# Block-sparse attention and a gated convolution feed-forward: the middle tap divided out, thirteen relus on another engine

## The chip, the core and the metric

The kernel runs on one core of a Trainium2 chip. A core has a matrix engine (TensorE, PE in the profile, with its weight loads as PEld), a vector engine (VectorE, DVE), a scalar engine that evaluates functions such as exp and tanh (ScalarE, ACT), a general engine (GpSimd, POOL) and a queue engine that here only issues transfers (SyncE, SP). Each engine works through its own list of instructions in the order in which they stand; an instruction that waits for another engine holds back all that stand behind it on its own. The metric is the device time of one execution in microseconds, smaller is better.

## What is computed

Attention over 4 batches, 8 heads, 768 positions and 64 values a head, with a mask of 32-wide blocks, and behind it a feed-forward part in which each of 1024 features is gated by a three-tap convolution along the positions:

```python
h = np.maximum(x @ w_in, 0.0)
conv_out = np.zeros_like(h)
for k in range(3):
    conv_out += conv_w[k][None, None, :] * hp[:, k:k + S, :]     # hp is h with a zero at each end
gate = 1.0 / (1.0 + np.exp(-conv_out))
return (h * gate @ w_out).astype(np.float32)
```

`x` is the attention's result, all heads side by side (512 values), `w_in` is 512 by 1024, `conv_w` 3 by 1024, `w_out` 1024 by 512.

## The kernel before

**Attention.** The work is cut into 144 units of eight 128x128 blocks of scores. A unit's scores are written by TensorE into one of two PSUM tiles `st` (line 746), ScalarE turns them into exponentials in one of eight SBUF tiles `pt` (line 757, the exp), and TensorE multiplies those with the values into one of two PSUM tiles `av` (line 779). A unit's scores can only be written when the exp of the unit two before has read that `st` tile. VectorE divides by the sums (`rcp`, `xtok`, lines 696 and 698), and the result is transposed into `xT`.

**Feed-forward.** The positions are cut into nine segments: seven of 384 positions (two to a batch, the last batch has one), one of 256 and one of 128. For a segment TensorE computes eight feature blocks of 128 features (F1, line 895: four matmuls of 384 columns a block) into one of two PSUM tiles `mix_65` and `mix_66`. A relu reads that tile and writes half of the positive part into the SBUF tile `hE`, either on ScalarE (line 915) or on VectorE (line 917); only then may TensorE write the tile anew. The same two `mix` tiles serve the transposes of queries and keys (lines 470 and 508, read out by the copies of lines 328 and 330) and the output blocks (F2, line 825, read out by copies into `o2s`).

The gate works on pairs of feature blocks, four pairs `pr` a segment, each in a buffer `m`: VectorE multiplies `hE` by each of the three taps (line 949, six instructions a pair, `cw` holds a tap of each feature as a column), adds the three products (line 959, two instructions), ScalarE takes the tanh of half of the sum, both blocks in one instruction (line 998), VectorE adds one (`g1`, line 1001) and multiplies with `hE` (`g2`, line 1006) into `gT`, which F2 reads. The factor one half in `hE` and the one in the tanh make that the sigmoid of the reference; `cw` holds the taps doubled. The segment of 128 positions does its taps on TensorE instead (line 970, tanh in line 975).

**What sets the order.** All operations are written as a graph, with the engines on which each may run. The string `ORDER` names each operation by two characters in the order in which it is put down, with a letter where a choice of engine was made and a character for each buffer; `put_down` follows it and plans nothing itself. So the string fixes the list of each engine, the engine of each relu, and the buffers.

The lines that the change and the steps below touch, shortened:

```python
i = nc.vector.tensor_scalar(out=m_t[cb.index][:, x, y, 0:w], in0=hE_t[heb.index][:, f0 + y, t0 + x:t0 + x + w],
                            scalar1=cw[:, x, f0 + y:f0 + y + 1], scalar2=None, op0=ALU.mult)      # L949
a1 = op("add", {"DVE": t_d2(2 * w)}, add(1, 0), due + 2.2, [m1, m0], uses=[cb])
a2 = op("add", {"DVE": t_d2(2 * w)}, add(1, 2), due + 2.3, [a1, m2], uses=[cb])
```

Of the kernel before, what the change touches and what calls it, by code (L numbers as in the profile page):

```python
# [32 lines left out]
iu18i08j8f38k4ix0iyizV8q18riviwViS4iTiUiV8v08wiA0iBiD1iE8s58x6iCAiFAi+0iW2o22p2qV22rV2u2002v22x2w8A18B7/08F086
878GiG08b8c8g8hiJ1iH8C78H0iXiIA8l8m8t18K18L8S08T8uiK2108yj08n1i/8oj122ViLV23Vj61j28M18U28z8X18Y8D8E8I8J90091
8Z3925j38N8O08ViM1951iP0969769d08WiQiNiOA8+9e8/939i194989j998P2j7iYj8j4iZj98Qj59a3iRVja9bje29f79k1jfjgjhji9n0
9o9p3jE1jbjs09g19s19t9u69h9l9x09yjt9z79mjF9F19q9r9G9v9w9A9K09L9B0jcjdjGjujj9H19M62F2G42C2D02Q2I2H2N2O12R32T2S
2Y2Z22y08222z2J18p8R9c9P19Q9R4jkjljHjIV29C02AV39Djv9I9U09Va019Ja1jN1jOjwA39W0a22jK0jLjMA1jPV0Gk63a50a6aa1jQ19N
abjT0jRk7k8jSVk9jUa75ac3jVA2/30032312Kaf0agak1alah7jZ1j+am1j/A9O9SjW09T9X9Yas0a31ata4a8jXa9ax1ayk31k4ke4kakb0L
kg9Z10H2BVjYVkm0knkf2LV4au6az4aC0aDaE0k00adk1aH1aeaIk2AaiajanaP0aQaJ2jm0jnkh9+ki2MVap2k5Vkcku1aU1aVaR5aW3kjjo
aZ0a+jpao0avawb21b3jy1aAaBaFaGaKaLa/7aqkv2EV32PV4kpkd1kob70b8kqkxaM3kk2+V0aNkwkl9E32U22Vin330jxarit349/b46jqA4  # L40
jzbf1bgb94jAjBbk0kI0aS1blaTaXaYaObh0krbm2jCA1bp1b0bqb1b5kJbu0bvb6ksky2WV02XVktbr5kzkAkBkC1babb0kD373833a3b13f
3c3d3ebw13mbC1bDbc035V1kEkKbH0kFbE3bIbM1bNkLkGV339A1bdkMV036VkO1kPbibJ7bO6kQVbR0bSkR0kSbT4kTVla2lblcldlebW1bj
bXbnbobsbY0kX1c20c3btkU0c71c8c42c95kYkVbxbykWAkZVbz2bAli3cc0cdbF1bGch1cibKl11ce1lfbLl2cp0cj3cqk+0bPbQbUbVbZb+0
cu1ljlklll3Vlmb/1lgc0cr7lnlhloc5l71cvk/l0Alq4cz0c6cacbcfcgcAcw6l40lplrlsltl5l8ckcE1clcFcm3l9VlucB0l6Aly0lzcnlB
lAlC3p3n03q23u3r3s3tcG4cJ0cKcs1ctcxcycClM0cL2lvcR1lG1cDcScW0cT5cHcXcY3cIlNcMcN0lHcUcVc/1d0d40d5lDjDbe03g13hjJ
c1bB3v23wcokHd17lwlxd66cZlIc+lOdc1ddde43iV2lElFd2lP3jVlQV1lJdh0lKA2didj5dm1dnm20m3d3do73E3B3F43J3G3xV3m4V0cO0
cPme1mfmgV3yVdr0d7dsm50m6dw1d8dxdt1m7Vmq1mrmsmtmud913oV23H3T3U33C13Idy03Y3V3W3Q3R23X43443df1mb1dE0dFdG2m80m9mc
dJ1mdAmaAdadKdgdO0dPdL6dQ3mh1mk0mlmidkdT1dUdldpdqdudvmjAd/0e0dzmn1dV4e41e5dA0dHdImoe15e67mpAe90eaeb1mvmy2mmVmz
mG3mImHmJmKmAdB2mBdCmCmO4lS0dMdNdRee1dSefdWdXlTe21e3lY1eg0mLdY3mwmx0mPlUej0eklZl+lVe7l/mDmQdZmRmMmS3DV3mEel2
m0A3e8er1esecew0edehexet6kN3kjr3K03LlR3Z1cQ1lWA0mFn01eieB1eCemn1mN3MV4mTey3eD4mUmV3NVeo0epmW0mXen0mYmZeG0eH  # L50
m+A4n2n3db3+3/V03zlLdDn4V140V3SV4eO1eP3Pd+nf0m1423leq2lX3O3An5ngnc1nd45A0eI5eQ7neAnhVnC0eT0eUeY1eZn90nan61n7
eV1e+0nEnDnbVn8AnFnu1f10f2euevf61f7nl0ezf32nmni1fe0f86nvnGnwnHnxnnVffeAnjeEnkVfj1fkeFeJeKfg3fl4nynzeL1nK2nLeM
nMnIeR1eSeWeXfo0fpno0e/f0ft1fuf4f5fq5f9nr1nsfv7fa0fB0fCnpfhfG1fHfifmfnfrfsfwfxfb2nNnAnJnqVnBntAfcnOfy3nS3fD1
fI0fL0fMfzn+1fN2fT1fUfE1fFo40nTnUnVnWfY0fJfZfKnPfV641eNfdfAf+3nXnQfOn/o5nRg11g2fPfQ0fW0fXf/g90g0g34gao0o6gb5g4
ge1gffRnYnZo7o1o2V2o8A3gg7gj0gkg5om0ong610MooA1gl1op1oqgc1gr1g7orVoK4oMoLoNoOov0gsgt0os1gdowoxAgw0otouAgxgB1gh
gCgioB0gmgnoCgy2oS0go2oDVgpfS3g8o9gqgD6oPgK0oy1ozgLgP1oH0oIgQgu0oAAgM3oE1gvgzgAgEoFgX0gYgR4oJAoGAoToUo+1o/p0p1
oVgFh31gN1gZ5gG3oQgHoWoXog0gOgSohgU0p62h4gI1h80h9gT0oiojp7oYp8oR1p9gVgJApap2h57okA0pq1prhh1g+pz0g/h61pApsApC3
h01ha1pBApbp3oa1h7hbobocodh1pEpDpFhd2pcpdp4oZpt0puhioeA1pvAgW0h2m/hep5pK4pLpw1pxhj0pyAhc0pk0plpmhf1pnhkhlpGpN
p+2p/hm3hnpMq1hgApoA3pHpOpS0pTpIpUpVpJpWpe1pfpgho0phhpApiA4ql0qmqnAqo1qpqi0qz1qAqjpPqqAqB1qkApppjolo3ofqE0qF
qr1qsqu1qvpQqCpRq60q7qDq0pXqtAqw3qG4qxq2q3qypYpZqc1qJ1qKqdqO0qL1qeqHq4qMq5q8q9qNqIqaA3qfqPqQqRqgA4qbqhqSA0qTS  # L60
qU0qVqWqXq+1qYA2qZSq/r0r1r2Ar3A
# [52 lines left out]
def kernel(  # L114
# [22 lines left out]
    SLOT_DMA = 3  # L137
    NF, NPE = 4, 5
    WHOLE = ()
# [29 lines left out]
    m_t = many(NCV, [128, 3, 2, 392], BF16, "m")  # L169
# [6 lines left out]
    cw = sb.tile([128, 3, NFFC], FP32, tag="cw", name="cw")  # L176
    ident = sb.tile([128, 128], BF16, tag="ident", name="ident")
# [195 lines left out]
    for s in range(NHE):  # L373
# [10 lines left out]
        op0=ALU.mult), T(8.5), [o_cwt], uses=[b_cw])  # L384

# [449 lines left out]
    def whole_gate(n, heb, gtb, base, W):  # L835

        got = []
        for f in range(NFFC):
            due = base + W * 0.6 * (f + 1) / 8
            cb = Buf(P_cv)  # L840
            rd = [relu[(n, f)], relu[(n - 1, f)]]

            def m_(x, cb=cb):
                return m_t[cb.index].rearrange("p x y s -> p x (y s)")[:, x, 0:S]

            def mul(x, f=f, m_=m_):
# [28 lines left out]
    for n, (b, g, tok, C, _) in enumerate(SEGS):  # L875
# [194 lines left out]
```

## Time and profile before

| what | value |
|---|---|
| three runs | 204.78, 205.15 and 205.30 us; median 205.15 |
| profiled execution, first to last instruction (span) | 202.8 us (its own device time is not on the page) |
| mean granted TensorE clock | 0.998 |
| PE busy | 196.8 us, 2708 matmuls |
| ACT busy | 189.7 us, 251 instructions |
| DVE busy | 181.8 us, 572 instructions |
| POOL busy | 57.5 us |

The median of the runs lies 2.35 us above the span. Busy time is the time in which an engine has at least one instruction in flight; instructions that follow each other on one engine overlap somewhat, so mean durations times counts come out above it. The row of a group gives, behind the bar, its busy time in us and the mean length of one in ns. A row of the timeline gives the start and the length in us, the engine, the line, what is written from what, and how many instructions in a row were merged.

### The profile page before, as it was taken

To read this page: it belongs to the slowest core of one execution; us is meant where nothing else is said; L and a number is where in the kernel's file an instruction comes from. 1 tells how busy PE (TensorE), PEld (TensorE's weight loads), DVE (VectorE), ACT (ScalarE), POOL (GpSimd) and SP (SyncE) were. 2 spreads that over 40 slices of the span, in tenths; PEclk is the share of its full clock that TensorE was granted. 3 is DMA by queue.
4 is the path that set the end of the run, shared out by engine and by line. 5 is a ranking of instruction groups with operands and counts; after the bars stand their busy time and mean duration, and the time that the engine had idled before them with its cause. 6 is when DMAs were issued, how large, how long until landed. Compare 5 with 4: busy or idle time off the path is not lost.

```text
span 202.8 us, 6814 instructions
## 1 busy us (share of the span) xinstructions
PE 196.8 (97%) x2708; PEld 153.9 (76%) x2708; DVE 181.8 (90%) x572; ACT 189.7 (94%) x251; POOL 57.5 (28%) x112
## 2 busy tenths in 40 slices
PE   7899999999999999999999999999999999999993
PEld 7799977986788777877688877876678877876742
DVE  7999989999999979999899988999899968999950
ACT  6999999999999999999999998999999989998842
POOL 8870568630520354202534328400000000000000
PEclk9999999999999999999999999999999999999999
DMA  6999999999998399956869699994321202001515
GB/s 143 177 223 207 182 135 132 167 171 151 155 122 129 61 141 154 213 106 132 133 108 159 82 197 218 135 176 115 124 72 24 41 14 68 13 10 60 204 63 202
DMA packets 53655, 25.96 MB, mean 128 GB/s; under 512 B 39616, under 2 KB 50584, under 8 KB 53624
## 3 DMA queue, kind: packets, MB, share of 16 engines
q0 software_dynamic: 19984, 11.24, 43.7%
q1 hardware_dynamic: 33208, 13.87, 34.6%
q8 instruction: 21, 0.34, 0.7%
q10 hardware_dynamic: 432, 0.43, 0.6%
q14 instruction: 10, 0.08, 0.1%
HBM read 23.08 MB, written 6.29 MB: 145 GB/s over the span
## 4 chain that ended last, share of the span: by engine, by line
PE 78%; ACT 15%; issue 3%; DVE 2%; DMA 1%; ACTq 0%
PE st L746 25%; PE mix L895 18%; PE mix L825 17%; PE av L779 14%; ACT pt L757 11%; DMA o2s<-in_k_dram 1%; DVE e L330 1%; ACT m L998 1%; PE mix L810 1%; PE st L825 1%; PE av L970 1%; ACT nat L328 1%; PE mix L508 1%; ACT hE L915 0%; ACT o2s L328 0%
## 5 line engine op out<-in xcount | busy, mean ns | idle before, releaser
L757 ACT ACTIVATE pt<-st 128x1024 bf16<-128x1024 f32 x144 | 140.6, 1039 | 1.8 <-PE st L746 0.9
L779 PE MATMUL av<-vt,pt 128*128 128x65 bf16 x1152 | 59.9, 193 | 0.2 <-DVE vt L330 0.2
L779 PEld LDWEIGHTS <-pt 128*128 128x128 bf16 x1152 | 52.3, 97 | 9.9 <-issue 0.3
L895 PE MATMUL mix<-xT,winb 128*128 128x384 bf16 (+2 forms) x288 | 53.6, 308 | 0.1
L949 DVE TENSOR_SCALAR m<-hE,cw 128x382 bf16<-128x382 bf16 (+2 forms) x192 | 49.3, 316 | 0.5 <-ACT hE L915 0.2
L825 PE MATMUL mix<-woutb,gT 128*128 128x512 bf16 x176 | 47.1, 379 | 0.3 <-DVE gT L1006 0.3
L746 PE MATMUL st<-o 88*128 88x128 bf16 (+1 forms) x240 | 43.9, 229 | 0.4 <-ACT pt L757 0.3
L746 PE MATMUL st<-o,e 88*128 88x128 bf16 (+1 forms) x228 | 43.4, 233 | 0.0
L746 PE MATMUL st<-e,o 88*128 88x128 bf16 (+1 forms) x224 | 42.3, 234 | 0.2 <-ACT pt L757 0.2
L746 PE MATMUL st<-e 88*128 88x128 bf16 (+1 forms) x208 | 40.9, 239 | 0.1
L746 PEld LDWEIGHTS <-o 88*128 88x128 bf16 x464 | 34.7, 97 | 7.7 <-issue 0.8
L746 PEld LDWEIGHTS <-e 88*128 88x128 bf16 x436 | 33.0, 97 | 7.1 <-issue 0.4
L959 DVE TENSOR_TENSOR m<-m 128x764 bf16<-128x764 bf16 (+2 forms) x64 | 33.5, 532 | 0.4
L895 PEld LDWEIGHTS <-winb 128*128 128x128 bf16 x288 | 24.0, 97 | 8.0 <-issue 0.5
L998 ACT ACTIVATE m<-m 128x764 bf16<-128x764 bf16 (+2 forms) x32 | 26.3, 829 | 0.5 <-DVE m L959 0.3
L825 PEld LDWEIGHTS <-gT 128*128 128x128 bf16 x184 | 15.0, 97 | 9.3 <-DVE gT L1006 0.5
L417 POOL COPY pace<-pt 1x1 bf16<-1x1 bf16 x24 | 6.2, 257 | 49.9 <-ACT pt L757 49.8
L1006 DVE TENSOR_TENSOR gT<-m,hE 128x764 bf16<-128x764 bf16 (+3 forms) x36 | 18.0, 510 | 0.5
L698 DVE TENSOR_TENSOR xtok<-av,rcp 128x384 bf16<-128x384 f32 (+2 forms) x36 | 18.2, 506 | 0.3
L915 ACT ACTIVATE hE<-mix 128x384 bf16<-128x384 f32 (+2 forms) x36 | 17.7, 507 | 0.7 <-PE mix L895 0.5
L240 POOL DMA_DIRECT2D nat<-in_q_dram x23 | 16.8, 733 | 3.2 <-issue 2.5
L917 DVE TENSOR_SCALAR hE<-mix 128x384 bf16<-128x384 f32 x28 | 15.3, 549 | 2.6 <-PE mix L895 2.2
(84 smaller groups left out, 157.4 us busy)
## 6 DMA issues: line engine op xcount, KB each, us to landing
out_dram<-o2s SPq DMA_DIRECT2D x23, 256.0 KB
vn<-in_v_dram POOLq DMA_DIRECT2D x16, 192.0 KB, 5.0
nat<-in_k_dram POOLq DMA_DIRECT2D x15, 192.0 KB, 4.7
nat<-in_q_dram POOLq DMA_DIRECT2D x7, 192.0 KB, 5.2
winb<-in_moe_w_in_dram POOLq DMA_DIRECT2D x2, 512.0 KB, 9.5
woutb<-in_moe_w_out_dram POOLq DMA_DIRECT2D x4, 256.0 KB, 8.2
nat<-in_q_dram POOLq DMA_DIRECT2D x8, 96.0 KB, 4.5
nq<-in_q_dram POOLq DMA_DIRECT2D x5, 96.0 KB, 5.2
```

Of the source, the lines that this page charges most:

```text
L240: return op(name, {eng: occ}, lambda e: on(e).dma_start(out=dst(), in_=src), prio, deps, dma=(kind, service), **kw)
L698: nm = op("norm", {"DVE": t_dps(128 * C)}, lambda e: nc.vector.tensor_tensor(out=xtok_t[xk.index][:, 0:C].rearrange("p c h d -> p h c d"), ...
L746: nc.tensor.matmul(out=st[:, 128 * x:128 * (x + n_)], lhsT=QK[kc % 2][s][0:88, 1, hh, kc // 2, :], rhs=QK[par][s][0:88, 0, hh, idx:idx + n ...
L757: nc.scalar.activation(out=pt_t[ptb.index], in_=st_t[stb.index], func=AF.Exp, bias=0.0, scale=0.125)
L779: nc.tensor.matmul(out=o[:, off:off + 65], lhsT=pt_t[ptb.index][:, 128 * x:128 * x + 128], rhs=V_t[vslot_b[P].index][:, hh, kc, 0:65], sta ...
L825: nc.tensor.matmul(out=acc(), lhsT=gT_t[gb.index][:, ffc, 128 * t:128 * t + 128], rhs=woutb[:, ffc, :], start=(ffc == 0), stop=(ffc == NFF ...
L895: nc.tensor.matmul(out=mix_t[hb.index][:, w1 * y:w1 * y + w1], lhsT=winb[:, fc, 128 * ffc:128 * ffc + 128], rhs=xT_t[xt_buf[n].index][:, f ...
L915: i = nc.scalar.activation(out=dst, in_=src, func=AF.Relu, bias=0.0, scale=0.5)
L949: i = nc.vector.tensor_scalar(out=m_t[cb.index][:, x, y, 0:w], in0=hE_t[heb.index][:, f0 + y, t0 + x:t0 + x + w], scalar1=cw[:, x, f0 + y: ...
L959: nc.vector.tensor_tensor(out=m[:, a_, :, 0:w], in0=m[:, a_, :, 0:w], in1=m[:, b_, :, 0:w], op=ALU.add)
L998: th = [op("tanh", {"ACT": t_act(2 * w) + 0.04}, lambda e, cb=cb, w=w: nc.scalar.activation(out=m_t[cb.index][:, 0, :, 0:w], in_=m_t[cb.in ...
L1006: i = nc.vector.tensor_tensor(out=gT_t[gtb.index][:, f0:f0 + 2, t0:t1], in0=m_t[cb.index][:, 0, :, 0:w], in1=hE_t[heb.index][:, f0:f0 + 2, ...
```

## The change

The taps are divided by the middle one once, in a new operation `cwr` of six small VectorE instructions (`ratios`). The middle tap's two multiplications of a pair go; the middle product is `hE` itself, added by `add_mid`; the tanh is given the middle tap as its scale. That scale differs from feature to feature, so it is read from a column of the new tile `cws`, and as one instruction takes one such column, the tanh becomes two instructions of half the length. `TINY` stands in for a middle tap near zero. Buffer `m` shrinks from three planes to two. The functions for a whole row at once (`whole_gate`) were not used, and go.

```diff
-    m_t = many(NCV, [128, 3, 2, 392], BF16, "m")
+    m_t = many(NCV, [128, 2, 2, 392], BF16, "m")
...
+    def ratios(e):
+        mid = cwr[:, 1]
+        nc.vector.tensor_tensor(out=cws, in0=cw[:, 1], in1=cw[:, 1], op=ALU.mult)
+        nc.vector.tensor_scalar(out=cws, in0=cws, scalar1=TINY * TINY, scalar2=TINY, op0=ALU.is_lt, op1=ALU.mult)
+        nc.vector.tensor_tensor(out=cws, in0=cws, in1=cw[:, 1], op=ALU.add)
+        nc.vector.reciprocal(out=mid, in_=cws)
+        nc.vector.tensor_tensor(out=cwr[:, 0:3:2], in0=cw[:, 0:3:2], in1=mid.unsqueeze(1).broadcast_to([128, 2, NFFC]),
+                                op=ALU.mult)
+        nc.vector.tensor_scalar(out=cws, in0=cws, scalar1=0.5, scalar2=None, op0=ALU.mult)
+
+    o_cwr = op("cwr", {"DVE": 0.5}, ratios, T(20), [o_cw])
...
-                        i = nc.vector.tensor_scalar(out=m_t[cb.index][:, x, y, 0:w],
+                        i = nc.vector.tensor_scalar(out=m_t[cb.index][:, x // 2, y, 0:w],
                                                     in0=hE_t[heb.index][:, f0 + y, t0 + x:t0 + x + w],
-                                                    scalar1=cw[:, x, f0 + y:f0 + y + 1], scalar2=None, op0=ALU.mult)
+                                                    scalar1=cwr[:, x, f0 + y:f0 + y + 1], scalar2=None, op0=ALU.mult)
...
+            def add_mid(e, f0=f0, cb=cb, heb=heb, t0=t0, w=w, n=n):
+                i = nc.vector.tensor_tensor(out=m_t[cb.index][:, 0, :, 0:w], in0=m_t[cb.index][:, 0, :, 0:w],
+                                            in1=hE_t[heb.index][:, f0:f0 + 2, 1 + t0:1 + t0 + w], op=ALU.add)
...
-                m1 = op("mul", {"DVE": 2 * t_d4(w)}, mul(1), due + 1.7, rd + [o_cw], alloc=[cb], uses=[heb])
-                m0 = op("mul", {"DVE": 2 * t_d4(w)}, mul(0), due + 2, rd + [o_cw], uses=[cb, heb])
-                m2 = op("mul", {"DVE": 2 * t_d4(w)}, mul(2), due + 2.1, rd + [o_cw], uses=[cb, heb])
-                a1 = op("add", {"DVE": t_d2(2 * w)}, add(1, 0), due + 2.2, [m1, m0], uses=[cb])
-                a2 = op("add", {"DVE": t_d2(2 * w)}, add(1, 2), due + 2.3, [a1, m2], uses=[cb])
-                th = [op("tanh", {"ACT": t_act(2 * w) + 0.04}, lambda e, cb=cb, w=w: nc.scalar.activation(
-                    out=m_t[cb.index][:, 0, :, 0:w], in_=m_t[cb.index][:, 1, :, 0:w], func=AF.Tanh, bias=0.0,
-                    scale=0.5), due + 2.8, [a2], uses=[cb])]
+                m0 = op("mul", {"DVE": 2 * t_d4(w)}, mul(0), due + 2, rd + [o_cwr], alloc=[cb], uses=[heb])
+                m2 = op("mul", {"DVE": 2 * t_d4(w)}, mul(2), due + 2.1, rd + [o_cwr], uses=[cb, heb])
+                a1 = op("add", {"DVE": t_d2(2 * w)}, add_mid, due + 2.2, [m0], uses=[cb, heb])
+                a2 = op("add", {"DVE": t_d2(2 * w)}, add(0, 1), due + 2.3, [a1, m2], uses=[cb])
+
+                def th_fn(e, cb=cb, w=w, f0=f0):
+                    for y in range(2):
+                        nc.scalar.activation(out=m_t[cb.index][:, 0, y, 0:w], in_=m_t[cb.index][:, 0, y, 0:w],
+                                             func=AF.Tanh, bias=0.0, scale=cws[:, f0 + y:f0 + y + 1])
+                th = [op("tanh", {"ACT": 2 * t_act(w) + 0.04}, th_fn, due + 2.8, [a2], uses=[cb])]
...
-15017A16ArLrM4n04o0/14s14t1g11j04p00q10V0p11V1hV11lV1kV4u11dV01iV4x04yrN0rOrPrQ4C14D4z2rRrSrTrUrVrWrXrY4H04I
+16018A17Argrh4o04p1014t14u1h11k04q00q11V0p12V1iV11mV1lV4v11eV01jV4y04zri0rjrkrl4D14E4A2rmrnrorprqrrrsrt4I04J
...
```

The order string is new throughout. It leaves the lists of TensorE, GpSimd and SyncE as they were, instruction by instruction and tile by tile. ScalarE's list loses 13 relus and has each of 32 tanhs in two halves. VectorE's has the 13 relus, the six small instructions and 64 multiplications fewer. Three places of VectorE's list matter below. In its rows `hE_116<-mix_66` is a relu of the block in `mix_66`, `m_119` and its neighbours are pair buffers, and `e`, `o`, `vt` are tiles of the attention.

First segment. VectorE before, from the division `xtok` on:

```order
L698 TENSOR_TENSOR xtok_104<-av_64,rcp_108 128x2x3x64
L917 TENSOR_SCALAR hE_116<-mix_65 128x384
L1001 TENSOR_SCALAR m_118<-m_118 128x2x382
L949 TENSOR_SCALAR m_119<-hE_116,cw 128x382 x2
L959 TENSOR_TENSOR m_119<-m_119 128x2x382
L949 TENSOR_SCALAR m_120<-hE_116,cw 128x382 x2
L330 COPY e_71<-mix_65 64x768
L330 COPY o_76<-mix_65 64x768
L949 TENSOR_SCALAR m_120<-hE_116,cw 128x382 x4
```

VectorE now, from the same `xtok` on:

```order
L711 TENSOR_TENSOR xtok_104<-av_64,rcp_108 128x2x3x64
L899 TENSOR_SCALAR hE_116<-mix_66 128x384
L899 TENSOR_SCALAR hE_116<-mix_65 128x384
L985 TENSOR_SCALAR m_118<-m_118 128x2x382
L899 TENSOR_SCALAR hE_116<-mix_66 128x384
L925 TENSOR_SCALAR m_119<-hE_116,cwr 128x382 x2
L933 TENSOR_TENSOR m_119<-m_119,hE_116 128x2x382
L925 TENSOR_SCALAR m_120<-hE_116,cwr 128x382 x2
L331 COPY e_71<-mix_65 64x768
L331 COPY o_76<-mix_65 64x768
L925 TENSOR_SCALAR m_120<-hE_116,cwr 128x382 x2
```

Both relus of `mix_66` stood on ScalarE. The first reads feature block 4, which TensorE fills after block 5 in `mix_65`; it now stands ahead of block 5's relu. The second reads block 7, the segment's last, and now stands ahead of the multiplications of `m_119` and of the copies out of `mix_65`.

Third segment, VectorE before, from `xtok` on:

```order
L698 TENSOR_TENSOR xtok_104<-av_64,rcp_108 128x2x3x64
L917 TENSOR_SCALAR hE_117<-mix_66 128x384
L390 TENSOR_SCALAR diag<-ident,cw 128x128 x3
L949 TENSOR_SCALAR m_121<-hE_117,cw 128x382 x6
L917 TENSOR_SCALAR hE_117<-mix_66 128x384
L959 TENSOR_TENSOR m_121<-m_121 128x2x382
```

The same stretch of VectorE's list now:

```order
L711 TENSOR_TENSOR xtok_104<-av_64,rcp_108 128x2x3x64
L899 TENSOR_SCALAR hE_117<-mix_65 128x384
L899 TENSOR_SCALAR hE_117<-mix_66 128x384
L403 TENSOR_SCALAR diag<-ident,cw 128x128 x3
L925 TENSOR_SCALAR m_121<-hE_117,cwr 128x382 x4
L899 TENSOR_SCALAR hE_117<-mix_66 128x384
L933 TENSOR_TENSOR m_121<-m_121,hE_117 128x2x382
L899 TENSOR_SCALAR hE_117<-mix_66 128x384
```

The relu of `mix_65` (block 0) came from ScalarE, as did the last row (block 5). TensorE fills block 1 in `mix_66` first and block 0 in `mix_65` second; VectorE now reads them in the other order.

Fifth segment, VectorE before, from the multiplications of its first pair on:

```order
L949 TENSOR_SCALAR m_119<-hE_116,cw 128x382 x6
L959 TENSOR_TENSOR m_119<-m_119 128x2x382 x2
L696 RECIPROCAL rcp_109<-av_63 128x6
L330 COPY vt_79<-vn_92 128x12x64
L698 TENSOR_TENSOR xtok_105<-av_63,rcp_109 128x2x3x64
L949 TENSOR_SCALAR m_120<-hE_116,cw 128x382 x2
L917 TENSOR_SCALAR hE_116<-mix_65 128x384
L949 TENSOR_SCALAR m_120<-hE_116,cw 128x382 x2
L949 TENSOR_SCALAR m_121<-hE_116,cw 128x382 x6
```

The same stretch now:

```order
L925 TENSOR_SCALAR m_119<-hE_116,cwr 128x382 x4
L933 TENSOR_TENSOR m_119<-m_119,hE_116 128x2x382
L941 TENSOR_TENSOR m_119<-m_119 128x2x382
L709 RECIPROCAL rcp_109<-av_63 128x6
L331 COPY vt_79<-vn_92 128x12x64
L899 TENSOR_SCALAR hE_116<-mix_66 128x384
L711 TENSOR_TENSOR xtok_105<-av_63,rcp_109 128x2x3x64
L899 TENSOR_SCALAR hE_116<-mix_66 128x384
L925 TENSOR_SCALAR m_120<-hE_116,cwr 128x382 x2
L899 TENSOR_SCALAR hE_116<-mix_65 128x384
L925 TENSOR_SCALAR m_121<-hE_116,cwr 128x382 x4
```

Both relus of `mix_66` are new here. Between the blocks that they read, TensorE fills `mix_66` once more (block 5, whose relu stays on ScalarE). The first reads block 3, the second block 7, which TensorE computes last; behind it stands the relu of `mix_65` (block 6), which stood here before without it.

121 lines of the change are left out of this document (46 added, 75 removed).

## The prediction

> **What bounds the kernel now.** I read the page's head and its chain of waits first, then who waits for whom on TensorE, then the groups by shape, and at last the timeline around the places where the order of VectorE's list changes.
>
> ```profile
> span 202.8 us, 6814 instructions
> PE 196.8 (97%) x2708; PEld 153.9 (76%) x2708; DVE 181.8 (90%) x572; ACT 189.7 (94%) x251; POOL 57.5 (28%) x112
> PE 78%; ACT 15%; issue 3%; DVE 2%; DMA 1%; ACTq 0%
> ```
>
> The chain of the end runs through TensorE for 78%, ScalarE for 15%, VectorE for 2%. So the engine that the change relieves most is hardly on the chain. What TensorE waits for after its start (its instruction, then what it waits for; us in all, count, longest):
>
> ```profile
> PE st L746 <- ACT pt L757: 0.4, 2, 0.3
> PE mix L825 <- DVE gT L1006: 0.3, 1, 0.3
> PE av L779 <- DVE vt L330: 0.2, 1, 0.2
> ```
>
> These are 0.9 us in all. TensorE's list is not changed, so **0.9 us is about the most that lighter neighbours can give**. What they can take has no such limit: TensorE works in order, and every relu that comes late holds a `mix` tile that it wants next.
>
> **The change part by part, as sums.** The groups by shape (busy us, mean ns behind the bar):
>
> ```profile
> L757 ACT ACTIVATE pt<-st 128x1024 bf16<-128x1024 f32 x144 | 140.6, 1039 | 1.8 <-PE st L746 0.9 <-PE av L779 0.2
> L949 DVE TENSOR_SCALAR m<-hE,cw 128x382 bf16<-128x382 bf16 x96 | 25.2, 321 | 0.2 <-ACT hE L915 0.2
> L917 DVE TENSOR_SCALAR hE<-mix 128x384 bf16<-128x384 f32 x28 | 15.3, 549 | 2.6 <-PE mix L895 2.2
> L915 ACT ACTIVATE hE<-mix 128x384 bf16<-128x384 f32 x28 | 13.7, 510 | 0.1
> L998 ACT ACTIVATE m<-m 128x764 bf16<-128x764 bf16 x16 | 13.4, 852 | 0.1
> L1001 DVE TENSOR_SCALAR m<-m 128x764 bf16<-128x764 bf16 x16 | 5.7, 359 | 0.9 <-ACT m L998 0.8
> L998 ACT ACTIVATE m<-m 128x512 bf16<-128x512 bf16 x4 | 2.5, 629 | 0.3 <-DVE m L959 0.3
> L1001 DVE TENSOR_SCALAR m<-m 128x512 bf16<-128x512 bf16 x4 | 1.1, 287 | 0.0
> ```
>
> VectorE: 64 multiplications go at 25.2/96 = 0.26 us, so -16.8; 13 relus come at 15.3/28 = 0.55, so +7.1; six small instructions, for which I take 0.2 each as an estimate below the 287 ns row, so +1.2. Net **-8.5 us**, hidden behind TensorE in any case. The middle product read from `hE` costs no more than from `m`: that addition keeps its count and its size.
>
> ScalarE: 13 relus go at 13.7/28 = 0.49, so -6.4. A tanh grows by (852-629)/(764-512) = 0.885 ns an element, so a half of 382 is 514 ns and a pair 1028 against 852: +0.18. The scale is now a column in memory, which no ScalarE row shows. From below it costs nothing. From above the nearest rows are VectorE's: `g1` with constants would be 359 - 382 x 0.286 = 250 ns at 382 elements, and the multiplication with a column is 321, so 71 ns. With it a pair costs +0.32. Over 32 pairs that is +5.8 to +10.2, net **-0.6 to +3.8 us** on ScalarE. I take the upper end, since VectorE pays for its column.
>
> The Trainium skill (ScalarE: Activation LUTs, What ACT_TABLE_LOAD costs) says that an ACTIVATE with constants takes 186 ns plus 0.833 ns an element, and that each column operand adds about 93 ns. The exp row agrees with the first part: 186 + 853 = 1039. By the second the 64 halves would cost 64 x 93 = 6.0 us for their columns instead of the 64 x 71 = 4.5 that I take; it speaks against the change, and would put ScalarE at +5.2.
>
> **Part by part, as an order.** Here lies the main cost. In the rows of the timeline stand start and busy time in us, then engine and line. First segment:
>
> ```profile
> 34.29 1.14 PE L895 MATMUL mix<-xT,winb 128*128 128x384 bf16 x6
> 35.02 0.55 DVE L917 TENSOR_SCALAR hE<-mix 128x384 bf16<-128x384 f32 x1
> 35.62 0.50 ACT L915 ACTIVATE hE<-mix 128x384 bf16<-128x384 f32 x1
> 35.96 0.53 DVE L949 TENSOR_SCALAR m<-hE,cw 128x382 bf16<-128x382 bf16 x2
> 36.00 0.50 PE L470 MATMUL mix<-ident,nat 128*128 128x128 bf16 x6
> 37.51 0.81 PE L895 MATMUL mix<-xT,winb 128*128 128x384 bf16 x4
> 38.76 0.50 ACT L915 ACTIVATE hE<-mix 128x384 bf16<-128x384 f32 x1
> 42.94 0.29 DVE L330 COPY o<-mix 64x256 bf16<-64x256 bf16 x1
> 43.29 0.38 PE L825 MATMUL mix<-woutb,gT 128*128 128x512 bf16 x1
> ```
>
> Block 4 is complete at 34.29+1.14 = 35.43. VectorE now takes it first (to about 35.9), then block 5, to 36.5; the key transposes at 36.00 need block 5's tile, so TensorE stops for 0.5. Block 7 is complete at 37.51+0.81 = 38.32, with the delay 38.8. Its relu now stands ahead of what VectorE began at 35.96, so VectorE idles from about 36.8 until 38.8 and begins that work at 39.3, 3.3 late. In the old run it took from 35.96 to the end of the copy `o<-mix` at 43.23, 7.3 us; four multiplications fewer make that 6.4, closed gaps perhaps 6.0. So that copy ends at 45.3 to 45.7. F2 followed it at 43.29 by 0.06, being the next into that tile. TensorE is then 2.0 to 2.4 late, the 0.5 included; the wait of 0.3 for `gT` behind it may go. **Term: +1.9** (1.0 to 2.4).
>
> Third segment:
>
> ```profile
> 76.34 0.56 DVE L917 TENSOR_SCALAR hE<-mix 128x384 bf16<-128x384 f32 x1 [0.29 <-PE mix L895]
> 76.99 0.53 ACT L915 ACTIVATE hE<-mix 128x384 bf16<-128x384 f32 x1
> 77.45 0.49 PE L895 MATMUL mix<-xT,winb 128*128 128x384 bf16 x2
> 79.98 0.81 PE L895 MATMUL mix<-xT,winb 128*128 128x384 bf16 x4
> 82.00 0.85 ACT L998 ACTIVATE m<-m 128x764 bf16<-128x764 bf16 x1
> ```
>
> Block 0 started on ScalarE as it was complete, at 76.99. Now VectorE waits for it and only then reads block 1, from 77.45 to 78.0; the F1 of 77.45 needs that tile: +0.6. Block 5 is complete at 80.79, now 81.4; behind its relu (0.55) stand two multiplications (0.5) and the addition that ends the first pair (0.55), so the tanh of 82.00 can start at 83.0, 0.4 beyond the delay, and exps queue behind it. **Term: +1.0** (0.5 to 1.5).
>
> Fourth segment:
>
> ```profile
> 110.15 0.86 ACT L998 ACTIVATE m<-m 128x772 bf16<-128x772 bf16 x1
> 110.92 0.50 ACT L915 ACTIVATE hE<-mix 128x384 bf16<-128x384 f32 x1
> 111.10 0.35 DVE L1001 TENSOR_SCALAR m<-m 128x772 bf16<-128x772 bf16 x1
> 111.77 0.98 PE L895 MATMUL mix<-xT,winb 128*128 128x384 bf16 x5
> ```
>
> The relu of 110.92 now stands behind the `g1` of 111.10, which waits for the tanh of 110.15, and that is 0.18 to 0.32 longer. The relu runs from about 111.6 to 112.1, the F1 of 111.77 waits: **+0.3** (0.1 to 0.5).
>
> Fifth segment:
>
> ```profile
> 126.35 1.14 PE L895 MATMUL mix<-xT,winb 128*128 128x384 bf16 x6
> 127.53 0.87 ACT L915 ACTIVATE hE<-mix 128x384 bf16<-128x384 f32 x2
> 128.80 0.32 DVE L330 COPY vt<-vn 128x768 bf16<-128x768 bf16 x1
> 128.34 1.47 PE L895 MATMUL mix<-xT,winb 128*128 128x384 bf16 x8
> 132.51 0.49 PE L895 MATMUL mix<-xT,winb 128*128 128x384 bf16 x2
> 133.28 0.60 PE L825 MATMUL mix<-woutb,gT 128*128 128x512 bf16 x2
> ```
>
> Block 3 is complete at 127.49 and was read at once by ScalarE. On VectorE it stands behind the copy `vt`, which ended at 129.12; with two multiplications fewer ahead of it the relu runs from 128.6 to 129.15. The F1 of 128.34 needs the tile: +0.85. Block 7 is complete at 133.00, now 133.85. VectorE waits for it from 129.6 on, four microseconds, then does its relu (0.5), two multiplications (0.5) and block 6's relu (0.55), to 135.4; F2 at 133.28 needs block 6's tile. **Term: +2.1**, the 0.85 included (1.2 to 2.5).
>
> **Tanhs elsewhere** (second and sixth segment, end): a pair costs ScalarE 0.32 more, a relu off it gives 0.49 back, and TensorE feels only what exceeds the gap between an exp and the scores that reuse its tile. I take **+0.9**, between 0 and 3.0 (nine pairs at 0.32).
>
> Sum 1.9 + 1.0 + 0.3 + 2.1 + 0.9 = +6.2, so a span of 209.0. The page gives no device time of its own; the runs' median, 205.15, lies 2.35 above the span, and I carry that over: **211.4 us**.
>
> **Rivals.** First, the waits of VectorE are absorbed: the list before waits little (L917's 2.6 us over 28 relus), and with 8.5 us of work less VectorE may catch up before TensorE asks. For the first segment's copy that could be half so; but the fifth segment's F2 follows the last F1 by 0.28 with two relus between, which no lead of VectorE shortens. Left would be 1.2 there, 0.6 in the third and little else, some of it against the 0.9 that can be gained: +1.3, 206.4.
>
> Second, the column is free on ScalarE. Then the queue's terms stay, and the tanhs give about nothing: +5.0, 210.2. For it speaks only that no ScalarE row shows the price; against it VectorE's 71 ns.
>
> Third, faster. If the new list meets its data on time, the 0.9 us of TensorE's waits shrink, most of all at the exps between 40 and 70 us, where the two relus taken off ScalarE in each segment give 0.98 against 4 x 0.18 = 0.72 for the tanhs with a free column: 202.8 - 0.9, so 204.3. It decides from the point where no relu on VectorE stands ahead of work that TensorE needs sooner, which the lists contradict in three segments.
>
> **How the numbers follow.** Forecast 0.64, first rival 0.14, second 0.14, third 0.05, and 0.03 for no change. A measurement of this kernel can tell about 0.3% from none. Faster 0.05, same 0.03, slower 0.92. The range takes the terms' lower ends (1.0+0.5+0.1+1.2+0 = 2.8, 208.0), goes below them towards the first rival, and up to the upper ends of most terms: 207.2 to 214.4. What lies outside is most of the first rival, the third, and a pile of upper ends.
>
> **What would show it.** Right: on VectorE a wait of about 2 us in line 899 near 37 and of about 4 us near 130; on TensorE waits for relus (lines 897 and 899 of the changed kernel, 915 and 917 now) in lines 470 and 895 and for VectorE's copy in the F2 near 43, some 5 us together against 0.9; tanhs of about 585 ns. Wrong: TensorE's waits below 2 us, or line 899 waiting no longer than L917 does now. If tanhs of 382 take 514 ns the column is free; if TensorE waits mostly for the exps, ScalarE is the loss and the queue is not.

## The result, and the profile after

The changed kernel takes 217.81 us (median of four runs, 217.58 to 218.74) against 205.13: a ratio of 1.0642 with a 95% interval of 1.061 to 1.0673, **slower by 12.7 us**. The forecast was 211.4, and its range ended at 214.4. The direction was right and the forecast loss, 6.2 us, half of what came. The profiled execution has a span of 215.8 us, 13.0 more than before.

The head of the changed kernel's page, and its chain of waits:

```profile
span 215.8 us, 6799 instructions
PE 202.0 (94%) x2708; PEld 155.0 (72%) x2708; DVE 175.5 (81%) x527; ACT 194.5 (90%) x270; POOL 57.9 (27%) x112
PE 47%; ACT 25%; DVE 12%; issue 8%; DMA 4%; POOL 3%; ACTq 0%; DVEq 0%
```

VectorE has 6.3 us less to do than before (8.5 forecast), and its share of the chain grew from 2% to 12%; ScalarE's went from 15% to 25%, TensorE's from 78% to 47%. What TensorE waits for, its startup left out (us in all, count, longest):

```profile
PE av L792 <- DVE xtok L711: 2.9, 2, 1.6
PE st L759 <- ACT pt L770: 2.2, 9, 0.3
PE mix L877 <- DVE hE L899: 1.8, 3, 0.9
PE mix L838 <- DVE hE L899: 1.2, 1, 1.2
...
PE av L792 <- ACT pt L770: 0.2, 1, 0.2
```

That is 8.3 us against 0.9. The larger stops in TensorE's timeline, with the two places ahead of the first of them:

```profile
36.05 0.22 PE L759 MATMUL st<-o 88*128 88x128 bf16 x1 [0.18 <-ACT pt L770]
36.55 0.49 PE L483 MATMUL mix<-ident,nat 128*128 128x128 bf16 x6
...
44.89 0.28 PE L792 MATMUL av<-vt,pt 128*128 128x65 bf16 x4 [1.64 <-DVE xtok L711]
81.70 0.48 PE L877 MATMUL mix<-xT,winb 128*128 128x384 bf16 x2 [0.52 <-DVE hE L899]
118.05 1.14 PE L877 MATMUL mix<-xT,winb 128*128 128x384 bf16 x6 [0.36 <-DVE hE L899]
136.15 1.46 PE L877 MATMUL mix<-xT,winb 128*128 128x384 bf16 x8 [0.88 <-DVE hE L899]
142.45 0.59 PE L838 MATMUL mix<-woutb,gT 128*128 128x512 bf16 x2 [1.20 <-DVE hE L899]
145.89 0.40 PE L792 MATMUL av<-vt,pt 128*128 128x65 bf16 x8 [1.23 <-DVE xtok L711]
```

TensorE's list is the same in both kernels, so its k-th matmul here is the k-th matmul there, and the difference of their starts is how late TensorE is:

| the same matmul | start before | start after | late | added at this stop |
|---|---|---|---|---|
| key transposes, first segment | 36.00 | 36.55 | 0.55 | 0.27 |
| `av`, first segment | 42.54 | 44.89 | 2.35 | 1.80 |
| F1, third segment | 77.45 | 81.70 | 4.25 | 0.68 |
| F1, fourth segment | 111.77 | 118.05 | 6.28 | 0.52 |
| F1, fifth segment | 128.34 | 136.15 | 7.81 | 1.04 |
| F2, fifth segment | 133.28 | 142.45 | 9.17 | 1.36 |
| `av` behind it | 135.32 | 145.89 | 10.57 | 1.40 |
| last matmul | | | 13.06 | |

The seven stops make 7.1 us, all of them at work of VectorE. The other 6.0 came in some two dozen steps of 0.1 to 0.5 us, 4.2 of them ahead of scores that wait for an exp to free their `st` tile. The first such step, 0.27 us at 36.05, stands just ahead of the key transposes: the tanh that starts at 33.07 takes 1.12 us in its halves, against 0.84 before, and the exps behind it are 0.28 late. VectorE's own list where its relus wait:

```profile
38.88 0.56 DVE L899 TENSOR_SCALAR hE<-mix 128x384 bf16<-128x384 f32 x1 [2.12 <-PE mix L877]
...
140.91 0.56 DVE L899 TENSOR_SCALAR hE<-mix 128x384 bf16<-128x384 f32 x1 [4.36 <-PE mix L877]
141.39 0.54 DVE L925 TENSOR_SCALAR m<-hE,cwr 128x382 bf16<-128x382 bf16 x2
141.84 0.55 DVE L899 TENSOR_SCALAR hE<-mix 128x384 bf16<-128x384 f32 x1
142.31 1.00 DVE L925 TENSOR_SCALAR m<-hE,cwr 128x382 bf16<-128x382 bf16 x4
...
144.75 0.19 DVE L709 RECIPROCAL rcp<-av 128x6 f32<-128x6 f32 x1
144.85 0.52 DVE L933 TENSOR_TENSOR m<-m,hE 128x764 bf16<-128x764 bf16 x1
145.28 0.55 DVE L711 TENSOR_TENSOR xtok<-av,rcp 128x384 bf16<-128x384 f32 x1
```

These are the waits that were forecast, of about 2 and about 4 us. Read on from the second: the relu of block 7 starts at 140.91; the relu of 141.84 behind it, block 6's, frees the tile for the F2 of 142.45; then come more products and sums, and only at 145.28 `xtok`, which frees the `av` tile for the matmuls of 145.89. One relu in the wrong place stops TensorE twice, which the run with this relu alone moved will show.

The groups that the change touches (busy us, mean ns | idle before):

```profile
L770 ACT ACTIVATE pt<-st 128x1024 bf16<-128x1024 f32 x144 | 139.9, 1034 | 7.6 <-PE st L759 6.0 <-POOL pace L430 0.4 <-PE av L792 0.2
L899 DVE TENSOR_SCALAR hE<-mix 128x384 bf16<-128x384 f32 x41 | 22.4, 553 | 12.7 <-PE mix L877 12.2
L982 ACT ACTIVATE m<-m,cws 128x382 bf16<-128x382 bf16 x32 | 17.8, 613 | 2.1 <-DVE m L941 2.1
L925 DVE TENSOR_SCALAR m<-hE,cwr 128x382 bf16<-128x382 bf16 x64 | 17.3, 322 | 0.1
```

The tanhs of all lengths are busy for 35.0 us against 26.3. In the row of the exps, 6.0 us of ScalarE's idle time wait for TensorE's scores, against 0.9 before: ScalarE is not the one that is late all the time. Each of the two falls behind the other in turn.

### The profile page after: what moved, and what is told of

It reads as the page before. It is cut to its first block, busy times and chain, and to the rows that moved or that the text cites. A ratio compares the mean times of both kernels' runs of the same rounds, so it can differ in the third digit from the quotient of the medians.

```text
span 215.8 us, 6799 instructions
## 1 busy us (share of the span) xinstructions
PE 202.0 (94%) x2708; PEld 155.0 (72%) x2708; DVE 175.5 (81%) x527; ACT 194.5 (90%) x270; POOL 57.9 (27%) x112
## 4 chain that ended last, share of the span: by engine, by line
PE 47%; ACT 25%; DVE 12%; issue 8%; DMA 4%; POOL 3%; ACTq 0%; DVEq 0%
PE st L759 15%; ACT pt L770 14%; PE mix L877 13%; PE mix L838 9%; ACT m L982 8%; PE av L792 7%; DMA nat<-in_k_dram 4%; DVE hE L899 3%; DVE m L925 3%; DVE m L933 2%; ACT o2s L329 1%; POOL nat L241 1%; POOL vn L241 1%; DVE xtok L711 1%; PE mix L823 1%
## 5 line engine op out<-in xcount | busy, mean ns | idle before, releaser
L982 ACT ACTIVATE m<-m,cws 128x382 bf16<-128x382 bf16 (+2 forms) x64 | 35.0, 605 | 2.5 <-DVE m L941 2.4
L925 DVE TENSOR_SCALAR m<-hE,cwr 128x382 bf16<-128x382 bf16 (+2 forms) x128 | 34.1, 317 | 0.4 <-ACT hE L897 0.2
L899 DVE TENSOR_SCALAR hE<-mix 128x384 bf16<-128x384 f32 x41 | 22.4, 553 | 12.7 <-PE mix L877 12.2
L430 POOL COPY pace<-pt 1x1 bf16<-1x1 bf16 x24 | 7.6, 315 | 56.4 <-ACT pt L770 56.3
L985 DVE TENSOR_SCALAR m<-m 128x764 bf16<-128x764 bf16 (+3 forms) x36 | 12.3, 343 | 8.2 <-ACT m L982 7.3
L941 DVE TENSOR_TENSOR m<-m 128x764 bf16<-128x764 bf16 (+2 forms) x32 | 17.1, 536 | 0.3
```

The source lines that it names most:

```text
L899: i = nc.vector.tensor_scalar(out=dst, in0=src, scalar1=0.5, scalar2=0.0, op0=ALU.mult, op1=ALU.max)
L925: i = nc.vector.tensor_scalar(out=m_t[cb.index][:, x // 2, y, 0:w], in0=hE_t[heb.index][:, f0 + y, t0 + x:t0 + x + w], scalar1=cwr[:, x, f ...
L941: nc.vector.tensor_tensor(out=m[:, a_, :, 0:w], in0=m[:, a_, :, 0:w], in1=m[:, b_, :, 0:w], op=ALU.add)
L982: nc.scalar.activation(out=m_t[cb.index][:, 0, y, 0:w], in_=m_t[cb.index][:, 0, y, 0:w], func=AF.Tanh, bias=0.0, scale=cws[:, f0 + y:f0 + ...
```

## The experiments

The change has three parts that can be taken apart: where the 13 relus stand in VectorE's list, that they are on VectorE at all, and the tanh in two halves with a scale from a column. All times are medians; before took 204.89 to 205.27 us beside them. In brackets stands the recorded ratio to the kernel before with its 95% interval, or, for the three runs that move one to three relus, the range of the executions.

**The relus put in place.** Eight moved relus change their places in VectorE's list. Five go behind work that does not need them, up to where their block is ready; one of the fourth segment and block 3's of the fifth go ahead of work behind which they stood; the third segment's first pair is swapped, for which the line that names the `hE` buffer has to follow the first of the two. The lists of the other four engines are those of the changed kernel. Three of the places in VectorE's list:

```diff
 L711 TENSOR_TENSOR xtok_104<-av_64,rcp_108 128x2x3x64
-L899 TENSOR_SCALAR hE_116<-mix_66 128x384
 L899 TENSOR_SCALAR hE_116<-mix_65 128x384
+L899 TENSOR_SCALAR hE_116<-mix_66 128x384
 L985 TENSOR_SCALAR m_118<-m_118 128x2x382
-L899 TENSOR_SCALAR hE_116<-mix_66 128x384
 L925 TENSOR_SCALAR m_119<-hE_116,cwr 128x382 x2
 L933 TENSOR_TENSOR m_119<-m_119,hE_116 128x2x382
 L925 TENSOR_SCALAR m_120<-hE_116,cwr 128x382 x2
+L899 TENSOR_SCALAR hE_116<-mix_66 128x384
 L331 COPY e_71<-mix_65 64x768
...
 L711 TENSOR_TENSOR xtok_105<-av_63,rcp_109 128x2x3x64
-L899 TENSOR_SCALAR hE_116<-mix_66 128x384
 L925 TENSOR_SCALAR m_120<-hE_116,cwr 128x382 x2
...
 L925 TENSOR_SCALAR m_120<-hE_116,cwr 128x382 x2
 L709 RECIPROCAL rcp_110<-av_64 128x6
+L899 TENSOR_SCALAR hE_116<-mix_66 128x384
 L933 TENSOR_TENSOR m_120<-m_120,hE_116 128x2x382
```

```diff
-            new = g == 0 and fg == 0
+            new = g == 0 and fg == (n == 2)
```

> The changed kernel with its moved relus still on VectorE, but nine relus (eight moved ones and a neighbour) put where their block is ready when VectorE gets there; the lists of the other four engines are unchanged. TensorE lost 13.0 us to the change: 3.6 waiting for VectorE's relus in lines 877 and 838, 3.2 waiting for xtok in line 792, and some 6 in small waits, mostly for exps. Queue theory (the place of the relus in VectorE's list): the first two go, some 6.8 us, and the time is near 211. ScalarE theory (the longer tanhs are the cause and VectorE's waits only follow them): it stays above 216. If the small waits for exps also come from VectorE, through tanhs that start late, it falls to about 207.

Measured: 210.75 us (1.0263, 1.0188 to 1.0338), 7.1 below the changed kernel. What TensorE still waits for there:

```profile
PE st L759 <- ACT pt L770: 1.9, 8, 0.3
...
PE mix L877 <- DVE hE L899: 0.3, 1, 0.3
PE av L792 <- DVE xtok L711: 0.3, 1, 0.3
PE av L792 <- ACT pt L770: 0.2, 1, 0.2
```

The waits for relus and `xtok` fell from 5.9 to 0.6 us, those for exps hardly changed (2.4 and 2.1). The place of the relus is worth 7.1 us, and the small waits for exps are another matter.

**One tanh a pair, relus as they are.** This leaves out the scale of each feature.

```diff
-                    for y in range(2):
-                        nc.scalar.activation(out=m_t[cb.index][:, 0, y, 0:w], in_=m_t[cb.index][:, 0, y, 0:w],
-                                             func=AF.Tanh, bias=0.0, scale=cws[:, f0 + y:f0 + y + 1])
+                    nc.scalar.activation(out=m_t[cb.index][:, 0, :, 0:w], in_=m_t[cb.index][:, 0, :, 0:w],
+                                         func=AF.Tanh, bias=0.0, scale=0.5)
```

> The changed kernel with its relus as they are, but one tanh a pair with the constant scale 0.5, which leaves the scale of each feature out. ScalarE has 32 instructions and some 8.7 us less to do (two halves step on by 2 x 501 ns, the one by 730). ScalarE theory: the small waits for exps go, some 6 us, and the time is near 212; if the longer tanhs are the cause of all, 206. Queue theory: the 6.8 us of waits for relus and xtok stay, so it is not below 211.

Measured: 213.63 us (1.0407, 1.0338 to 1.0476), 4.2 below the changed kernel. Its waits for `xtok` (3.1 us) and relus (3.3) stood as before; those for exps fell from 2.2 to 0.3. So the place of the relus and the longer tanhs each cost their part.

**Both edits at once.**

> Both at once: the relus put in place, and one tanh a pair with a constant scale (the scale of each feature is left out). If queue and tanhs are all there is, this is at the time of the kernel before or a little under it, 204.3 to 206. If it stays above 207, something third costs: the small setup instructions, the buffers, the relus' own time on VectorE.

Measured: 206.14 us (1.0059, 1.0025 to 1.0094). The two gains add up: 217.81 - 7.1 - 4.2 = 206.5. Some 1 us remains. The profiled execution took 207.24, 1.1 more than the median, and is 2.7 us late at its end. Of these, 1.43 come at one stop near 54 us: VectorE, early now, waits 1.78 us for the transfer of the next keys, with the copies out of a `mix` tile behind it. 0.41 come at the `xtok` of the first segment and 0.51 at the F1 of the fifth:

```profile
PE mix L877 <- DVE o2s L331: 1.3, 1, 1.3
...
PE mix L877 <- DVE hE L899: 0.3, 1, 0.3
...
PE av L792 <- DVE xtok L711: 0.2, 1, 0.2
```

The last two are there in every trace with the relus in place, and in none with the relus back on ScalarE; together they fit the 1 us. Whether the shorter executions lack the stop near 54 us is not shown, as their traces were not kept.

**The relus back on ScalarE.** The changed arithmetic in the order of the kernel before, its middle multiplications left out.

> The changed arithmetic with the order string of the kernel before: all 13 relus on ScalarE at their old places, VectorE 64 multiplications lighter, the tanhs in two halves with a scale from a column. ScalarE theory: ScalarE has 8.7 us more than before and nothing back, so 210 to 214. Queue theory alone: VectorE has no relu in a bad place, so 205 to 207.

Measured: 210.59 us (1.0263, 1.02 to 1.0325), the same as with the relus in place on VectorE. Taking 13 relus off ScalarE gave nothing, even in good places. Two rows of each kernel, first with the relus in place, then with them back:

```profile
PE 200.5 (96%) x2708; PEld 154.4 (74%) x2708; DVE 176.5 (84%) x527; ACT 193.8 (93%) x270; POOL 57.9 (28%) x112
L770 ACT ACTIVATE pt<-st 128x1024 bf16<-128x1024 f32 x144 | 140.1, 1034 | 4.2 <-PE st L759 2.5 <-POOL pace L430 0.3 <-PE av L792 0.2
```

```profile
PE 200.9 (96%) x2708; PEld 155.5 (75%) x2708; DVE 170.7 (82%) x514; ACT 197.0 (94%) x283; POOL 57.3 (27%) x112
L770 ACT ACTIVATE pt<-st 128x1024 bf16<-128x1024 f32 x144 | 140.7, 1048 | 1.8 <-PE st L759 1.2 <-PE av L792 0.2
```

The 3.2 us that ScalarE no longer works are 2.4 us more in which it waits ahead of its exps. The same scores (at 73.05 in the kernel before) wait for the same exp, in the changed kernel and with the relus back:

```profile
76.61 0.22 PE L759 MATMUL st<-e 88*128 88x128 bf16 x1 [0.19 <-ACT pt L770]
```

```profile
74.97 0.22 PE L759 MATMUL st<-e 88*128 88x128 bf16 x1 [0.19 <-ACT pt L770]
```

Counted as in the table, TensorE loses 0.35 us there in the changed kernel, 0.36 with the relus in place, 0.36 with them back, and 0.02 with one tanh. All the steps ahead of scores make 4.2, 3.9, 5.0 and 0.2 us in these four. They come from the tanhs, wherever the relus are.

**The relus moved, nothing else.** The arithmetic of the kernel before, with the changed kernel's order.

> The arithmetic of the kernel before (three multiplications a block, one tanh a pair with a constant scale) with the changed kernel's order: only the 13 relus move to VectorE, to the same places. ScalarE has 4.8 us less to do than before. Queue theory: the relus' places alone cost what they cost in the run with one tanh (some 8), and a little more since VectorE is busier: 213 to 216. If ScalarE were the cause and VectorE only followed, 203 to 206.

Measured: 219.22 us (1.0677, 1.0629 to 1.0726), beyond what either expected: 14.3 us lost, though ScalarE has less to do than before. Compared with the run that has one tanh (213.63), the 64 multiplications that VectorE keeps cost another 5.6 us (4.8 to 5.6 by the executions of both whose mean granted clock was 0.997 or more). TensorE waits longer at the same stops:

```profile
36.60 0.49 PE L470 MATMUL mix<-ident,nat 128*128 128x128 bf16 x6 [0.38 <-DVE hE L917]
46.09 0.33 PE L779 MATMUL av<-vt,pt 128*128 128x65 bf16 x4 [2.79 <-DVE xtok L698]
```

**Halves with a constant scale, relus in place.** As above with `scale=0.5` in each half.

> The changed kernel with its relus in place and each tanh in two halves, but with the constant scale 0.5 in place of the column (the scale of each feature is left out). It lies between the run in place with one tanh (206.14) and the one in place with halves and columns (210.75). If the column carries two thirds, as a line through the two tanh lengths of the kernel before (409 ns for 382 values, against 501 measured with the column) says, then about 207.6; if the split itself is the cost, 210 or more; if only the column is, 206.

Measured: 207.16 us (1.0109, 1.0058 to 1.016). The split costs 1.0 us of time, the column 3.6. The rows of its halves, and of those with the column (relus in place in both):

```profile
L982 ACT ACTIVATE m<-m 128x382 bf16<-128x382 bf16 x32 | 14.8, 525 | 0.4 <-DVE m L941 0.3
```

```profile
L982 ACT ACTIVATE m<-m,cws 128x382 bf16<-128x382 bf16 x32 | 17.7, 614 | 0.3 <-DVE m L941 0.3
```

A column makes an instruction 614 - 525 = 89 ns longer, 2.9 us for 32 by the busy times, which is 91 each. The Trainium skill (ScalarE: Activation LUTs, What ACT_TABLE_LOAD costs) gives about 93 ns for an operand of that kind; this run agrees. The same section says that ACTIVATEs that follow each other overlap by about 93 ns. By that a split costs one more fixed part of 186 less 93; by the busy times here it is 2 x 14.8/32 - 13.4/16 = 0.09 us a pair, which agrees too.

**Only the fifth segment's relus in place.** Those of blocks 3 and 7 are moved; block 6's then stands right without a move.

> The changed kernel with only the three relus of the fifth segment (blocks 3, 6, 7) put in place. In the trace of the changed kernel TensorE lost 1.04, 1.36 and 1.40 us there. If these waits are lost for good, the time falls by 3.8, to about 214.0; if the prediction's term was right, by 2.1, to 215.7; if they are made up later anyway, it stays at 217.8.

Measured: 216.15 us (214.57 to 216.3), which looks like 1.7 gained. But three of its four executions had a mean granted clock of 0.992, the one at 1.0 took 214.57. The changed kernel's three executions at 0.998 and above took 217.58 to 217.94. Compared at the same clock the gain is 3.1 us, by one execution, or 2.5 by those near 0.99 (216.23 against a single 218.74), and in its profiled execution 0.50 remains of the 3.8 that the three stops had added. What the clock does is told in the last section.

**Only the first segment's relus in place.**

> The changed kernel with only the two relus of the first segment (blocks 4 and 7) put in place. TensorE was 2.4 us late behind this place, 1.8 of them in one wait for xtok. If that is lost for good, the time falls by 2 to 2.4, to about 215.6; if later slack takes it in, it stays near 217.8.

Measured: 216.35 us (215.88 to 217.47), 1.5 gained. The stop of 1.64 fell to 0.25, and the one at the key transposes went, 1.65 us together by the starts of the matmuls. In the profiled execution, the slowest of the four, a new stop stands a little later, the same as in the run with both edits:

```profile
55.13 0.48 PE L877 MATMUL mix<-xT,winb 128*128 128x384 bf16 x2 [1.18 <-DVE o2s L331]
```

Here a transfer, for which VectorE waits 1.51 us, sets when it goes on, and what it gained ahead of that is partly given back.

**One relu alone, block 7 of the fifth segment.** Only the last of the moves shown above.

> The changed kernel with one relu moved: block 7 of the fifth segment, seven rows later in VectorE's list. VectorE waited 4.4 us for this block, and behind it TensorE lost 1.36 us in the F2 of line 838 and 1.40 in line 792 waiting for xtok. If both are that one relu's, the time falls by 2.7, to 215.1. By the prediction's account the relu of block 7 cost 1.25 in all (2.1 less 0.85), which gives 216.6. If the waits are shared with blocks 3 and 6, it stays above 217.

Measured: 216.0 us (215.55 to 216.99), all four executions at a clock of 0.990 to 0.992. The changed kernel's one execution at such a clock (0.990) took 218.74, which makes 2.7 us for this one relu, though with a single execution on that side. The trace is plainer: the stops of 1.36 and 1.40 are gone, and the one of 1.04 ahead of them, which is block 3's, stands as it was.

**One tanh, and halves with a constant, both with the relus back on ScalarE.**

> The changed arithmetic in the order of the kernel before (all 13 relus on ScalarE at their old places) and one tanh a pair with the constant scale 0.5 (the scale of each feature is left out). What is left of the change is that VectorE is 64 multiplications lighter, and six small instructions. If a lighter VectorE gives something by itself, up to the 0.9 us that TensorE waited for its neighbours: 204 to 204.9. If it sets nothing, 204.9, the time before. Together with the run that has the relus back and the tanhs in halves with columns (210.59) it gives the price of the tanhs where no relu has moved: 5 to 6 us of the 8.7 that ScalarE's list is longer; if the price were mostly the moved relus', under 2.

> As the run before in this call, but each tanh in two halves with the constant scale 0.5 (the scale of each feature is left out): ScalarE's list is 32 x 92 ns = 2.9 us longer instead of 8.7. If TensorE loses the same share of each microsecond that ScalarE gets, near a third of the way from the run with one tanh to 210.59, so about 206.8; if ScalarE has room for the first microseconds and none for the later ones, nearer to 205.5.

Measured: 205.37 us (1.0016, 0.9984 to 1.0048) and 205.93 us (1.0046, 1.0009 to 1.0082). 64 multiplications less on VectorE are worth nothing while the relus stay on ScalarE: in the profiled execution TensorE gains 0.44 us at the F2 of 48.14, the wait for `gT`, and loses 0.72 at the F1 of 52.51, behind the same transfer, for which VectorE waits 1.21 us. With the relus on ScalarE the split costs 0.6 us and the column 4.7: ScalarE has room for the first 2.9 us of longer work and little for the next.

**The relus in place, with the arithmetic of the kernel before.**

> The arithmetic of the kernel before (three multiplications a block, one tanh a pair), with only the 13 relus moved to VectorE, but put in place as in the first run. ScalarE has 4.8 us less to do, VectorE 7 more. If relus in good places cost nothing and ScalarE's relief counts, 204 to 205; if VectorE, which then works over 90% of the time, is too late for TensorE by itself, 207 or more.

Measured: 209.91 us (1.0245, 1.0188 to 1.0302). With all multiplications left on it VectorE works 187.9 of 208.0 us, and TensorE waits for it in good places too, for relus and `xtok`:

```profile
PE mix L895 <- DVE hE L917: 1.8, 3, 0.8
PE st L746 <- ACT pt L757: 1.3, 3, 0.7
...
PE av L779 <- DVE xtok L698: 0.9, 1, 0.9
```

So once the relus are on VectorE the 64 multiplications do count: 209.91 against 206.14 in place, 3.8 us.

No run was faster than the kernel before.

| | one tanh | halves, constant | halves, column |
|---|---|---|---|
| relus on ScalarE | 205.37 | 205.93 | 210.59 |
| relus on VectorE, in place | 206.14 | 207.16 | 210.75 |
| relus on VectorE, as changed | 213.63 | | 217.81 |

## Why the prediction was wrong, step by step

Two steps failed. The tanhs elsewhere, forecast at 0.9 us, cost 4.2 to 5.2, because the relus taken off ScalarE were counted against them and gave nothing back. And the fifth segment's term ended at the F2, where 1.40 us more came at the next `xtok`.

**What bounds the kernel** was right: TensorE is the bound, and with the relus left on ScalarE the lighter VectorE gave nothing (205.37).

**The order** was the right mechanism in the right places: 5.3 forecast, 7.1 measured. The steps of the table that are gone or smaller in the run in place, with two more of the third segment, make 6.8.

- First segment, 1.9 forecast, 1.6 measured: 0.27 at the key transposes and 1.38 of the 1.80 at `av`; the rest, 0.42, stays in place. The key transposes start when worked out, at 36.55, but half of their lateness was the tanh's. VectorE's idle 2 us came as worked out. What TensorE met late was not the copy that frees the tile of F2 but `xtok`, for matmuls that stand earlier in TensorE's list. This step followed the lateness along VectorE's list to one reader and did not look for an earlier one. Its size came out near all the same, since the same late list is behind both readers.
- Third segment, 1.0 forecast, 1.3 measured: 0.68 at the F1, 0.51 at 88.67, ahead of scores that wait for an exp, and 0.15 right behind. The second is the late tanh of that term: it starts at 86.59, after 0.61 us of waiting for VectorE's addition, and in the run in place neither that wait nor the step is there.
- Fourth segment, 0.3 forecast, 0.52 measured.
- Fifth segment, 2.1 forecast, 3.3 measured: 0.54 of the 1.04 at the F1 (0.85 forecast; 0.50 stays in place), 1.36 at the F2 behind block 6's relu (1.25 forecast), and 1.40 that the term did not have. **The step that failed is that it ended at F2.** VectorE's list was then still late, and `xtok`, later in it, stopped TensorE a second time. The run with that one relu moved shows both stops to be its own.

**The tanhs elsewhere are the step that failed most.** Their price on ScalarE was about right, even a little high: 0.32 us a pair forecast, (35.0 - 26.3)/32 = 0.27 by the busy times; within it the column was taken too low (71 ns against 91) and the split too high (176 against 90, since mean lengths count the overlap of neighbours twice). The relus' credit was too high, in part for the same reason: 0.49 us each forecast, 3.2/13 = 0.25 by ScalarE's busy time with the relus back and in place. So ScalarE's busy time rose by 4.8 us (189.7 to 194.5), past the 3.8 at the forecast's upper end. But even that credit was worth nothing to TensorE. Wrong was the sentence that TensorE feels only what exceeds a gap, with the 0.49 us of each relu given back. Measured, 8.7 us more of tanh cost 4.2 us with the relus as changed, 4.6 in place and 5.2 with them on ScalarE; and the relus taken off ScalarE returned nothing (210.75 against 210.59). The steps ahead of scores say why: a tanh stands between two exps at a given place, and a relu that went from another place cannot shorten the stop that the tanh makes there. At the first of them, TensorE loses its 0.27 at 36.05; the relu that went had stood behind, at 35.62 in ScalarE's list before, and in its place ScalarE waits 0.49 us for TensorE's scores at 37.48. The upper end of this term, 3.0, was built on nine pairs, where all 32 count.

The sign that was to tell the queue from ScalarE, for whom TensorE waits, was of little use: the listed waits for exps are 2.4 of 8.3 us, and the tanhs cost 4.2 to 4.6 of the 12.7.

So the loss is made up of three parts, taken one after the other: 205.37 with a lighter VectorE, +0.8 for the relus on VectorE in good places, +4.6 for the halves and columns, +7.1 for the places, 217.8 in all. The 0.8 by itself is not clear of the noise (the intervals of its two runs, 0.9984 to 1.0048 and 1.0025 to 1.0094, overlap), but the stops of 0.41 and 0.51 us that come with it are in the traces; with all multiplications left on VectorE it is 4.6 (209.91 against 205.27). The first rival, that the waits are absorbed, is refuted by the run in place; the second, a free column, by the 3.6 to 4.7 us that it costs; the third, faster, by every run.

## What to carry to other kernels

An operation moved to another engine's list is paid for by its place: if its input may be late, everything behind it in that list is late as well, and each consumer down the list has to be followed until the list has caught up, not just the first. Work added to a nearly full engine between the instructions that feed the bound counts there and then; in this kernel work taken off it elsewhere was no credit against it. A scale that differs by row was not free on ScalarE, 0.09 us an instruction, even where it saved a whole multiplication on VectorE, which was not the bound.

## What the runs showed of the hardware that was not expected

**TensorE's clock can fall to half behind a stop of under two microseconds.** In some executions the stop near 44 us is followed by a drop. The windows of one microsecond of the run with block 7 moved (us, PE busy and so on by engine, then the granted clock in front of the DMA share):

```profile
45.00:46.00 1.00, 0.88 (x11) 0.60 (x11) 0.97 (x5) 0.98 (x2) 0.00 (x0) 1.00 1.38 172
46.00:47.00 1.00, 1.00 (x12) 0.76 (x11) 0.97 (x5) 0.00 (x0) 0.00 (x0) 0.75 2.42 147
47.00:48.00 1.00, 1.00 (x18) 0.94 (x17) 1.00 (x3) 0.51 (x1) 0.00 (x0) 0.50 2.01 152
48.00:49.00 1.00, 1.00 (x18) 0.94 (x16) 0.58 (x3) 1.00 (x3) 0.00 (x0) 0.50 2.35 154
49.00:50.00 1.00, 1.00 (x13) 0.87 (x11) 1.00 (x3) 0.85 (x3) 0.00 (x0) 0.54 0.65 36
50.00:51.00 1.00, 1.00 (x15) 0.63 (x13) 0.97 (x3) 1.00 (x2) 0.00 (x0) 1.00 1.47 179
```

The missing shares, 0.25 + 0.50 + 0.50 + 0.46, make 1.71 us, which at half clock is 3.4 us of time. The stop, 1.82 us long there, ends at 45.12; the 0.75 of the second row puts the fall near 46.5, some 1.4 us later. The same came behind stops of 1.75 and 2.79 us in two other runs, there 0.2 and 0.1 us after their ends, and not behind the 1.64 us in the changed kernel's profiled execution, nor behind 1.83 us in the run with one tanh. That the stop causes it is not shown: of the kernel before, whose trace has no such stop, two executions of 208.89 and 210.46 us also had a mean granted clock of 0.992 and 0.983, and their traces were not kept. The Trainium skill (TensorE: Matmul & The Clock Gate, What's actually happening) tells of a free-running window of about 3.4 us by which the clock is set, half or full, and of a fall after an idle window; the 3.4 us and the half agree, but ahead of two of the drops TensorE stood still for only 1.75 and 1.82 us, little more than half of such a window.

**A stop costs more than its row says.** The idle times printed at the stops are 1.64, 0.52, 0.36, 0.88, 1.20 and 1.23 us, and what TensorE was later behind each is 1.80, 0.68, 0.52, 1.04, 1.36 and 1.40: always 0.16 or 0.17 more. A matmul is shown busy after the next one could have started: those at 36.05 and 36.11 start 0.06 us apart, and each is shown busy for 0.22. So a sum of waits is too small by 0.16 for each stop, and short stops hardly show at all. With 0.16 for each of the 16 listed stops the 8.3 us become 10.9, of a loss of 13.0.
